# Counting every transfer in the planner's estimate of the DMA queue, turning the first x + h first, and turning part of the attention scores by DMA

## The chip, the cores and the metric

The kernel runs on one core of one Trainium2 chip. Its time is the device time of one execution in microseconds (us). The kernel before was timed three times: 1010.28, 1007.97 and 1010.57 us, median 1010.28 us. One execution was recorded with a profile; durations below come from that one.

The core has these engines: PE (TensorE) multiplies matrices and writes to PSUM, which is read by DVE (VectorE) and ACT (ScalarE); POOL (GpSimd) does a few casts at the start; SP (SyncE) computes nothing, it issues every transfer (DMA) of this kernel. Each engine takes its own instructions strictly in the order in which they were written, and waits at an instruction until what that instruction needs is there.

## The reference

There are eight batches of 3136 rows (keys and queries at once) and 256 columns.

```python
scores = (1/S) * z @ z.T            # z: 8 x 3136 x 64, so scores are symmetric
attn   = maximum(scores, 0) ** 2
x      = u * (attn @ v)             # u, v: 8 x 3136 x 256
h      = (x.T @ U @ V).T            # U: 3136 x 32, V: 32 x 3136
y      = x + h
out    = y + maximum(y @ w_ch1, 0) @ w_ch2    # 256 -> 1024 -> 256
```

The scores of a batch are a 3136 x 3136 symmetric matrix. A block of it that is needed with keys and queries exchanged can therefore be had in two ways: compute it a second time on PE, or transpose (turn) the block that is there.

## The kernel before, in words

**Tiling.** 3136 rows are 24 tiles of 128 rows and one tail of 64. Four tiles make a group of 512, so a batch has six full groups (0 to 5) and a seventh item for the tail. `items` (L56) lists (batch, group): 56 items, t = 7b + g. The kernel works on one item after the other; item (b,g) is the attention output of query group g of batch b.

**What an item does on PE.** `av_stream` (L501) multiplies the scores of all 24 key tiles with v, block by block: `lhs(h, q, jt)` fetches the piece of the score block (b, g, jb), jb = jt // 4. Between these matmuls `emit` (L857) mixes other work at given places: score blocks of later items (`score_burst`), the mixer of an item that lies eight items back (`ch1_part`, `ch2_stream`), and `u2_unit` (L661), which makes y = x + h of the item seven back. `av_end` (L599) adds the part of the 64 tail keys. PE therefore always has work of three kinds: attention, scores, mixer. `pair` (L159, the matmul is L164) issues two matmuls of 64 rows, one on each half of PE's rows.

**Score blocks.** A block is 512 keys by 512 queries, 128 partitions x 2048 in bf16, and lives in one of 20 buffers (`take_block`, `give_block`). For query group g the blocks with J >= g are computed (two bursts of a pair of 64x512 matmuls, `score_pairs` L349; then ReLU with scale, `rectify` L317, on ACT or DVE; then `square` L313 on DVE). The blocks with J < g are turned by DMA from the block (b, J, g) computed earlier (`issue_turn` L336, the transfer is L341). The scores of the 64 tail keys against 512 queries are computed too: one burst ("last") for every two groups, in `last_sb`. Those of the tail queries against all keys are made in `score_small` (L416).

**x + h.** `u2_unit` makes y on DVE in 32 bits (L708), casts it to bf16 (`cast` L181, on whichever of ACT and DVE is free first by the plan), and turns it by DMA (`x_turn` L621, transfer L624) into `u2T`, which `ch1_part` reads one item later.

**The planner.** The order of all instructions is fixed when the program is written, by a plan kept beside it. `clock` counts PE's work (one unit for a pair of 256 columns); `free_at` holds when ACT, DVE and SP will be free by this plan; `hold` keeps work back until its due time, and `run_held` (L109) issues it. Turns that could go wait in `ready_turns`; `run_held` issues one when `free_at["sp"] <= now`, in the order of the group that needs it (J first). Before the change only the turns of blocks are booked on SP (34 units each, L345); loads, stores and the turns of x + h are not. A turn that is still in `ready_turns` when its block is wanted is issued there and then, by the loop in `lhs` (L509 to L513).

**SP's queue.** On SP stand, in the order in which they were written: at the end of item t the store of the output (`ch2_out`, L832), which waits for the last DVE result of the mixer of that item; at the start of the next item the load of u (L278, or L283 for the tail's 64 rows) and one or two loads of v (L227) or of z; then turns of blocks (L341) and the turn of x + h (L624). Only the order on SP and the data that a transfer needs decide when it starts: where in PE's stream it was written does not hold it.

Of the kernel before, what the change touches and what calls it, by code (L numbers as in the profile page):

```python
# [18 lines left out]
def kernel(  # L19
# [79 lines left out]
    unturned = {}  # L99
    ready_turns = []  # L100

    def book(eng, ready, cost):
        free_at[eng] = max(free_at[eng], ready) + cost
        return free_at[eng]

    def hold(due, f):
        held.append((due, len(held), f))

    def run_held(now=None):  # L109
        now = clock[0] if now is None else now  # L110
        while True:
            ripe = [h for h in held if h[0] <= now]
            if not ripe:
                break
            h = min(ripe, key=lambda e: (e[0], e[1]))
            held.remove(h)
            h[2]()
        while ready_turns and free_at["sp"] <= now:
            issue_turn(min(ready_turns, key=lambda e: (e[0], e[2], e[1])))
# [77 lines left out]
    def load_tail(raw, c0, a, n):  # L197

        for h in range(2):
            nc.sync.dma_start(out=raw[h * TAIL : (h + 1) * TAIL, c0 : c0 + n], in_=a[NF * P : S, :])  # L200


    def load_z_piece(b, t0, n, raw, tail=True):
        m = min(n, NF - t0)
        nc.sync.dma_start(  # L205
            out=raw[:, : m * dqk].rearrange("p (t d) -> p t d", d=dqk), in_=rows_of(z[b])[:, t0 : t0 + m, :]
        )
        if n > m and tail:
            load_tail(raw, m * dqk, z[b], dqk)
            load_tail(raw, n * dqk, v[b], D)  # L210
# [15 lines left out]
    def load_v_piece(b, k, raw):  # L226
        nc.sync.dma_start(  # L227
            out=raw.rearrange("p (t d) -> p t d", d=D), in_=rows_of(v[b])[:, k * GT : (k + 1) * GT, :]
        )

    def v_copy(b, k, raw, copy):
# [42 lines left out]
    def load_u(b, g):  # L274
        g0, gw = groups[g]
        t = pool.tile([P, GT, D], FP32, name="u_sb", bufs=2)
        if gw >= P:
            nc.sync.dma_start(  # L278
                out=t[:, : gw // P, :],
                in_=rows_of(u[b])[:, g0 // P : (g0 + gw) // P, :],  # L280
            )
        else:
            nc.sync.dma_start(out=t[:gw, 0, :], in_=u[b, g0 : g0 + gw, :])  # L283
        u_sbs[b, g] = t


    def z_turn_dma(b):
        nc.sync.dma_start_transpose(
            out=zzTs[b], in_=z_bfs[b].rearrange("p t c d -> p (t c d)")
        )  # L290

    def z_turn(b, t0, copy):
# [17 lines left out]
    def half(zzT, jj, c0, n):  # L310
        return zzT.rearrange("p t c -> p (t c)")[jj * dqk : (jj + 1) * dqk, c0 : c0 + n]

    def square(a, cost=6.3):  # L313
        book("dve", clock[0], cost)
        nc.vector.tensor_tensor(out=a, in0=a, in1=a, op=ALU.mult)  # L315

    def rectify(dst, src):  # L317

        ready = clock[0] + 3
        if max(free_at["dve"], ready) + 8 < max(free_at["act"], ready):  # L320
            nc.vector.tensor_scalar(  # L321
                out=dst, in0=src, scalar1=scale, scalar2=0.0, op0=ALU.mult, op1=ALU.max
            )
            return book("dve", ready, 11.2)
        nc.scalar.activation(out=dst, in_=src, func=AF.Relu, scale=scale)  # L325
        return book("act", ready, 8.7)

# [5 lines left out]
    def made_twice(b, g, J):  # L333
        return b == 0 and (g <= FIRST or J == g - 1)

    def issue_turn(e):  # L336
        ready_turns.remove(e)
        J, g, b = e
        src = blocks[b, g, J]
        blocks[b, J, g] = take_block()  # L340
        nc.sync.dma_start_transpose(  # L341
            out=blocks[b, J, g][1].rearrange("p j (q c) -> p (j q) c", c=P),
            in_=src[1].rearrange("p j c -> p (j c)"),
        )
        book("sp", clock[0], 34)  # L345
        if unturned.pop(src[0]):
            free_blocks.append(src[0])

    def score_pairs(jobs):  # L349

        made = []
        for b, g, job in jobs:
            zzT = zzTs[b]
            k, ps = take_ps()
            if job == "last":
                keys, cols = [NF, NF], [groups[g + jj][0] for jj in range(2)]
            else:
                J, h = job
                keys, cols = [J * GT + 2 * h + jj for jj in range(2)], [groups[g][0]] * 2
            pair(  # L360
                k,
# [4 lines left out]
                        dict(  # L366
                            out=ps[:, jj, :],
                            lhsT=half(zzT, jj, keys[jj] * P, P),
                            rhs=half(zzT, jj, cols[jj], GW),
                            start=True,  # L370
# [4 lines left out]
                ],  # L375
                GW,
            )
            if job == "last":
                lasts[b, g // 2] = pool.tile([P, 2, GW], BF16, name="last_sb")
                made.append((lasts[b, g // 2], k, ps, None, None))  # L380
                continue
            if h == 0:
                blocks[b, g, J] = take_block()
            made.append(
                (
# [9 lines left out]
    def score_finish(made):  # L395
        for dst, k, ps, turn, key in made:
            if turn:
                J, g, b = turn
                unturned[blocks[b, g, J][0]] = False
# [10 lines left out]
            hold(done, finish)  # L410

    def score_burst(jobs):
        score_finish(score_pairs(jobs))


    def score_small(b, g):  # L416
# [7 lines left out]
        for p0 in range(0, npair, per):  # L424
            n = min(per, npair - p0)
            pk, ps = take_ps()
            for k in range(n):
# [7 lines left out]
                                out=ps[:, jj, k * gw : (k + 1) * gw],  # L435
                                lhsT=half(zzT, jj, (2 * (p0 + k) + jj) * P, P),
                                rhs=half(zzT, jj, g0, gw),
# [63 lines left out]
    def av_stream(b, g, box):  # L501
        def lhs(h, q, jt):
# [12 lines left out]
            if jb >= g or made_twice(b, g, jb):  # L515
                while squared.get((b, g, jb), 0) < 2:
                    run_held(min(h[0] for h in held))
                return t[h, j, q * P : (q + 1) * P]

# [32 lines left out]
    def av_small(b, g):  # L552
# [3 lines left out]
        for jt in range(NT):  # L556
            c = jt % 2
            for h in range(2):
                nc.tensor.matmul(  # L559
                    out=ps[c * hp : c * hp + rows, h, :D],  # L560
                    lhsT=smalls[b][h * hp : (h + 1) * hp, jt, :],
                    rhs=v_bfs[b][h * hp : (h + 1) * hp, jt, :],
                    start=(jt < 2),
                    stop=(jt >= NT - 2),
                    tile_position=(h * hp, c * hp),
                )
# [32 lines left out]
    def av_end(b, g, box):  # L599

        last = lasts[b, g // 2]
        for a in range(2):
# [6 lines left out]
                        out=four(box["ps"])[:, q, :],  # L609
                        lhsT=last[h, g % 2, q * P : (q + 1) * P],  # L610
                        rhs=v_bfs[b][h, NF, :],
# [9 lines left out]
    def x_turn(b, g, turned):  # L621
# [4 lines left out]
            in_=xs[b, g][:rows, :n, :].rearrange("p q d -> p (q d)"),  # L626
        )


# [31 lines left out]
    def u2_unit(b, g, turn=True):  # L661
# [51 lines left out]
        def turned():  # L713
            u2Ts[b, g] = u2T_tile()
            x_turn(b, g, u2Ts[b, g])

        def down():
            hold(cast(x, o[:rows, :n, :], n * D) + 2, turned)

        hold(done - 3, down)  # L720

# [101 lines left out]
    def ch2_out(b, g, acc):  # L823
# [7 lines left out]
        dst = rows_of(out[b])[:, t0 : t0 + n, :] if rows == P else out[b, t0 * P : S, None, :]  # L831
        nc.sync.dma_start(out=dst, in_=o)  # L832
        if (b, g) in o_blocks:
            give_block(o_blocks.pop((b, g)))
# [71 lines left out]
    def jobs_of(b, g):  # L906
        js = [J for J in range(NQ) if J >= g or made_twice(b, g, J)]
        j = [(b, g, (J, h)) for J in js for h in range(2)]
        if g % 2 == 0:
            j.append((b, g, "last"))  # L910
# [5 lines left out]
    def load_U():  # L916
        entry, raw = stage_block()
        nc.sync.dma_start(out=raw[:, : NF * R].rearrange("p (t r) -> p t r", r=R), in_=rows_of(moe_U))
        nc.sync.dma_start(out=raw[:TAIL, NF * R : NT * R], in_=moe_U[NF * P :, :])

        def casts():
# [6 lines left out]
    def load_w(k):  # L928
        def step(i):
# [4 lines left out]
            else:  # L934
# [3 lines left out]
                )  # L938
                dst = w2_bf[:, i * GT : (i + 1) * GT, :].rearrange("p t d -> p (t d)")

            def casts(entry=entry, raw=raw, dst=dst):
# [8 lines left out]
    def load_V(i0):  # L950
        n = P // 4

        def step(i):
            entry, raw = stage_block()
            w = n * NF + (S - NF * P if i == 3 else 0)
            for c in range(NREP):
                nc.sync.dma_start(out=raw[c * R : (c + 1) * R, :w], in_=moe_V[:, i * n * NF : i * n * NF + w])

            def casts(i=i, entry=entry, raw=raw):
# [103 lines left out]
    for b in range(B):  # L1063
        for g in range(NQ):
# [8 lines left out]
            elif b == 0 and g == 0:  # L1073
                todo[0] += new[4:]
            else:
                todo[t] += new
# [6 lines left out]
    for t in range(n_items):  # L1083
# [30 lines left out]
        if t <= NG:  # L1114
            hold(clock[0] + 60, lambda t=t: load_u(*items[t + 1]))
        if b_next < B and g_now == 2:
            while spare:
# [18 lines left out]
        full = mix and mix[1] < NQ  # L1136
        if av and g_now == NQ - 1:
            qm.append((55, 2, False, lambda: score_small(att[0], NQ)))
        if av and full:
# [36 lines left out]
        if av and u2i:  # L1176
            if u2i[1] == 0:
                qm.append((8, 1, False, lambda: t1_all(u2i[0])))
            qm.append((34 if u2i[1] == 0 else 40, 1, False, lambda: u2_unit(*u2i)))

# [72 lines left out]
```

## Time and profile before

| what | us |
|---|---|
| runs without profile | 1010.28, 1007.97, 1010.57 |
| the profiled execution | 1010.08 |
| its span, first to last instruction | 1008.3 |
| PE busy | 986.7 |
| DVE busy | 653.6 |
| ACT busy | 520.2 |

The profile names a group of instructions by its line in the kernel, its engine, and "out<-in" by the names of the tiles. "idle before, releaser" says how long the engine stood still before that group and what ended it. PE is busy nearly all of the span. In the steady part a batch takes 121.66 us: the same pieces of the chain that ended last come back at 224.32, 345.98, 467.64 us and so on. The first batch has no mixer work; the last items have no scores.

### The profile page before, as it was taken

Reading aid. Unit: us, or ns where it says so; the run is one execution under the profiler, and the core shown is the slowest. Engines: PE = TensorE matmul, PEld = TensorE weight load, DVE = VectorE, ACT = ScalarE, POOL = GpSimd, SP = SyncE. Lnnn points to the kernel's source line nnn. Section 1 sums busy time; section 2 is a strip of 40 time slices with the busy share of each in tenths; the row PEclk is TensorE's granted clock in tenths of the full one; section 3 lists DMA queues with packets and bytes.
Section 4 is the critical chain, followed back from the end, with each engine's and each line's share of the span. In section 5 each row is a group of like instructions: output and inputs, shape, how many; then the busy total and the mean of one; then the engine's idle time right before and its main releaser. Section 6 shows DMA issues by size and latency. Waiting matters only on the chain.

```text
span 1008.3 us, 35337 instructions
## 1 busy us (share of the span) xinstructions
PE 986.7 (98%) x16179; PEld 784.7 (78%) x16179; DVE 653.6 (65%) x820; ACT 520.2 (52%) x599; POOL 17.2 (2%) x24
## 2 busy tenths in 40 slices
PE   6999899999999999999999999999999999999997
PEld 3898688877787777778777877778777777787776
DVE  5986675668666685666756677566776667653453
ACT  6896653357524573355733456444653356522453
POOL 4100000000000000000000000000000000000000
PEclk9999899999999999999999999999999999999999
DMA  7997998478966799568995789846798577873142
GB/s 247 187 257 178 235 170 166 130 166 186 213 142 165 152 199 218 149 145 181 182 209 157 129 193 188 210 127 140 179 216 185 137 158 143 160 127 88 45 103 94
DMA packets 337061, 167.84 MB, mean 166 GB/s; under 512 B 312336, under 2 KB 315408, under 8 KB 336912
## 3 DMA queue, kind: packets, MB, share of 16 engines
q1 hardware_dynamic: 336912, 165.59, 76.3%
q8 instruction: 126, 2.06, 0.8%
q14 instruction: 23, 0.19, 0.1%
HBM read 62.56 MB, written 25.69 MB: 88 GB/s over the span
## 4 chain that ended last, share of the span: by engine, by line
PE 94%; DVE 2%; ACT 2%; DMA 1%; issue 0%; POOL 0%; SPq 0%; POOLq 0%; ACTq 0%
PE ps L164 92%; PE ps L559 1%; DVE blk L315 1%; ACT blk L793 1%; PE ps L635 1%; DMA blk<-in_v_dram 1%; ACT blk L325 1%; PE ps L843 0%; DMA u2T<-x_bf 0%; DMA stage<-in_v_dram 0%; POOL z_bf L213 0%; SPq L205 0%; DVE blk L321 0%; DVE out_sb L708 0%; DVE blk L830 0%
## 5 line engine op out<-in xcount | busy, mean ns | idle before, releaser
L164 PEld LDWEIGHTS <-blk 64*128 64x128 bf16 x12288 | 617.6, 94 | 153.6 <-POOLq L154 8.7
L164 PE MATMUL ps<-v_bf,blk 64*128 64x256 bf16 x9216 | 617.2, 270 | 2.3 <-DVE blk L315 1.8
L325 ACT ACTIVATE blk<-ps 128x1024 bf16<-128x1024 f32 x324 | 323.4, 1027 | 337.2 <-PE ps L164 334.0
L315 DVE TENSOR_TENSOR blk<-blk 128x1024 bf16<-128x1024 bf16 x352 | 237.7, 701 | 34.1 <-ACT blk L325 33.4
L164 PE MATMUL ps<-u2T,w_bf 64*128 64x512 bf16 (+1 forms) x1792 | 239.1, 351 | 4.3 <-DMA u2T<-x_bf 3.5
L164 PE MATMUL ps<-w_bf,blk 64*128 64x256 bf16 x3072 | 193.7, 269 | 0.2
L790 DVE TENSOR_SCALAR blk<-ps 128x1024 bf16<-128x1024 f32 x96 | 115.7, 1205 | 102.3 <-PE ps L164 102.3
L793 ACT ACTIVATE blk<-ps 128x1024 bf16<-128x1024 f32 (+1 forms) x128 | 107.3, 847 | 82.4 <-PE ps L164 74.1
L164 PE MATMUL ps<-zzT 64*128 64x512 bf16 (+1 forms) x944 | 143.5, 342 | 1.9 <-ACT zzT L305 1.7
L164 PEld LDWEIGHTS <-w_bf 64*128 64x128 bf16 x1792 | 91.6, 94 | 35.1 <-DMA u2T<-x_bf 3.8
L592 DVE TENSOR_TENSOR x_bf<-ps,u_sb 128x1024 bf16<-128x1024 f32 x48 | 58.8, 1224 | 63.0 <-PE ps L164 62.9
L708 DVE TENSOR_TENSOR out_sb<-ps,x_bf 128x1024 f32<-128x1024 f32 (+1 forms) x49 | 54.3, 1107 | 53.7 <-PE ps L164 53.6
L830 DVE TENSOR_TENSOR out_sb<-ps,out_sb 128x1024 f32<-128x1024 f32 x42 | 51.3, 1222 | 18.3 <-PE ps L164 18.3
L164 PEld LDWEIGHTS <-zzT 64*128 64x128 bf16 x944 | 43.9, 95 | 9.2 <-ACT zzT L305 2.2
L325 ACT ACTIVATE last_sb<-ps 128x1024 bf16<-128x1024 f32 x23 | 23.5, 1024 | 26.5 <-PE ps L164 26.5
L321 DVE TENSOR_SCALAR blk<-ps 128x1024 bf16<-128x1024 f32 x24 | 29.4, 1224 | 10.3 <-PE ps L164 8.7
L186 DVE CAST x_bf<-out_sb 128x1024 bf16<-128x1024 f32 x33 | 22.8, 690 | 0.5
L186 DVE CAST v_bf<-stage 128x1024 bf16<-128x1024 f32 (+1 forms) x34 | 21.2, 626 | 0.0
L164 PE MATMUL ps<-t_sb,V_bf 64*128 64x256 bf16 x200 | 20.8, 269 | 0.0
L164 PE MATMUL ps<-v_bf,last_sb 64*128 64x256 bf16 x192 | 18.6, 269 | 0.0
L830 DVE TENSOR_TENSOR blk<-ps,blk 128x1024 f32<-128x1024 f32 x6 | 7.3, 1225 | 16.0 <-PE ps L164 15.9
L578 ACT COPY u_sb<-ps 64x512 f32<-64x512 f32 x8 | 4.7, 582 | 23.9 <-PE ps L559 23.9
(67 smaller groups left out, 249.5 us busy)
## 6 DMA issues: line engine op xcount, KB each, us to landing
u_sb<-in_u_dram SPq DMA_DIRECT2D x48, 512.0 KB, 5.0
stage<-in_v_dram SPq DMA_DIRECT2D x42, 512.0 KB, 6.0
out_dram<-out_sb SPq DMA_DIRECT2D x42, 512.0 KB, 3.1
stage<-in_z_dram SPq DMA_DIRECT2D x7, 512.0 KB, 5.5
blk<-in_v_dram SPq DMA_DIRECT2D x6, 512.0 KB, 7.2
out_dram<-blk SPq DMA_DIRECT2D x6, 512.0 KB, 2.6
blk<-in_moe_w_ch_dram SPq DMA_DIRECT2D x4, 512.0 KB, 5.8
stage<-in_z_dram SPq DMA_DIRECT2D x7, 256.0 KB, 5.7
```

What stands on the lines that cost most here:

```text
L164: ins = nc.tensor.matmul(**args)
L186: nc.vector.tensor_copy(out=out, in_=in_)
L315: nc.vector.tensor_tensor(out=a, in0=a, in1=a, op=ALU.mult)
L321: nc.vector.tensor_scalar(out=dst, in0=src, scalar1=scale, scalar2=0.0, op0=ALU.mult, op1=ALU.max)
L325: nc.scalar.activation(out=dst, in_=src, func=AF.Relu, scale=scale)
L559: nc.tensor.matmul(out=ps[c * hp : c * hp + rows, h, :D], lhsT=smalls[b][h * hp : (h + 1) * hp, jt, :], rhs=v_bfs[b][h * hp : (h + 1) * hp ...
L592: nc.vector.tensor_tensor(out=xs[b, g][:rows, :n, :], in0=four(box["ps"])[:rows, :n, :], in1=u_sbs[b, g][:rows, :n, :], op=ALU.mult,)
L635: nc.tensor.matmul(out=pt[c * R : (c + 1) * R, 0, :D], lhsT=U_bf[:rows, it, :], rhs=xs[b, g][:rows, q, :], start=(it < NREP), stop=(it + N ...
L708: nc.vector.tensor_tensor(out=o[:rows, :n, :], in0=four(ps)[:rows, :n, :], in1=x, op=ALU.add)
L790: nc.vector.tensor_single_scalar(out=r, in_=ps[:, :, :gw], scalar=0.0, op=ALU.max)
L793: nc.scalar.activation(out=r, in_=ps[:, :, :gw], func=AF.Relu)
L830: nc.vector.tensor_tensor(out=o, in0=acc, in1=o, op=ALU.add)
```

## The change: what it does

1. **Every transfer is booked on SP in the plan.** `queued(kb, turned)` adds 15 units per 512 KB of an ordinary transfer and 17 per 256 KB of a turned one to `free_at["sp"]`; it is called beside each load, store, z turn and x + h turn. `run_held` issues a block's turn only when SP is free by this larger sum; a turn that is still held when its block is wanted goes by the loop in `lhs`, as before.
2. **First x + h.** For group 0 of each batch `u2_unit` stands at place 22 of the item and not at 34, its cast is always on DVE and right behind the sum, and while `urgent` is filled no block's turn is issued.
3. **Tail keys by turning.** For batches 1 to 7 the three "last" bursts fall away. `score_small` of a batch is made in the item before the batch begins, and `last_turn` turns 24 x 64 of its columns into `last_sb` by one DMA at the start of the batch (12 pieces of 128 x 128). The order of the tiles in `attn_small` is changed so that the halves fit (`place_of`).
4. **A quarter of each diagonal block by turning.** In the block (b, g, g), `split` for all but the first four groups of batch 0, the second burst computes 256 columns and not 512, with ReLU and square over half as much; the missing quarter is turned by a DMA of 4 pieces of 128 x 128 inside the block. That turn goes through `ready_turns` with J = g. In `lhs` PE's stream needs it from the third tile of the block on.

```diff
+    def queued(kb, turned=False):
+        book("sp", clock[0], kb * (17 / 256 if turned else 15 / 512))
...
-        while ready_turns and free_at["sp"] <= now:
+        while ready_turns and free_at["sp"] <= now and not urgent:
             issue_turn(min(ready_turns, key=lambda e: (e[0], e[2], e[1])))
...
     def issue_turn(e):
         ready_turns.remove(e)
         J, g, b = e
         src = blocks[b, g, J]
+        if J == g:
+            nc.sync.dma_start_transpose(
+                out=flat_of(src)[:, 3 * GW :].rearrange("p (n c) -> p n c", c=P),
+                in_=flat_of(src)[:, GW : 2 * GW],
+            )
+            book("sp", clock[0], 12)
+            split_turned.add((b, g))
+            return
...
+                if split(b, g, J) and h:
+                    width = hw
+                    cols = [c + hw for c in cols]
...
+    def score_finish_split(flat, k, ps, h, key):
+        if h:
+            done = rectify(
+                flat[:, 2 * GW : 3 * GW].rearrange("p (j c) -> p j c", c=hw), ps[:, :, :hw], 0.5
+            )
+            a, cost = flat[:, 2 * GW : 3 * GW], 3.7
...
+        def finish():
+            square(a, cost)
+            squared[key] = squared.get(key, 0) + 1
+            if not h:
+                b, g, J = key
+                hold(clock[0] + 7, lambda: ready_turns.append((J, g, b)))
...
+    def last_turn(b):
+        lasts[b] = last_tile()
+        nc.sync.dma_start_transpose(
+            out=lasts[b], in_=smalls[b][:, :NF, :].rearrange("p t c -> p (t c)")
+        )
+        book("sp", clock[0], 26)
...
+                if split(b, g, jb):
+                    while j >= 2 and q < 2 and (b, g) not in split_turned:
+                        if (g, g, b) in ready_turns:
+                            issue_turn((g, g, b))
+                        else:
+                            run_held(min(h[0] for h in held))
...
-            hold(done - 3, down)
+        if g == 0:
+            urgent.append((b, g))
+            nc.vector.tensor_copy(out=x, in_=o[:rows, :n, :])
+            hold(book("dve", done, 6.3) - 6, turned)
+        else:
+            hold(done - 3, down)
...
         nc.sync.dma_start(out=dst, in_=o)
+        queued(n * rows)
...
-        if g % 2 == 0:
+        if g % 2 == 0 and b == 0:
             j.append((b, g, "last"))
...
+        if g_now == 0 and t:
+            last_turn(att[0])
...
-        if av and g_now == NQ - 1:
-            qm.append((55, 2, False, lambda: score_small(att[0], NQ)))
+        if av and t == NQ - 2:
+            qm.append((55, 2, False, lambda: score_small(0, NQ)))
+        if av and g_now == NQ - 1 and b_next < B:
+            qm.append((55, 2, False, lambda: score_small(b_next, NQ)))
...
-            qm.append((34 if u2i[1] == 0 else 40, 1, False, lambda: u2_unit(*u2i)))
+            qm.append((22 if u2i[1] == 0 else 40, 1, False, lambda: u2_unit(*u2i)))
```

## The prediction

> **What bounds the kernel now.** I read the page's busy times first, then its costliest groups, the windows around the one long wait of PE, and last the timelines of SP and PE over one late item of a batch.
>
> Page before: engines, granted clock, and the groups of PE with waits (busy, mean ns of one | idle before, releaser).
>
> ```profile
> PE 986.7 (98%) x16179; PEld 784.7 (78%) x16179; DVE 653.6 (65%) x820; ACT 520.2 (52%) x599; POOL 17.2 (2%) x24
> PEclk9999899999999999999999999999999999999999
> ...
> L164 PE MATMUL ps<-u2T,w_bf 64*128 64x512 bf16 (+1 forms) x1792 | 239.1, 351 | 4.3 <-DMA u2T<-x_bf 3.5
> ...
> L164 PE MATMUL ps<-zzT 64*128 64x512 bf16 (+1 forms) x944 | 143.5, 342 | 1.9 <-ACT zzT L305 1.7
> ```
>
> PE bounds the kernel: less work on PE is time won, and a wait put into PE is time lost in full, since no other slack follows it. The 3.5 us is the only long wait after the start, the first turned x + h. The windows around it (us, PE, PEld, DVE, ACT, POOL busy, clock, DMA share, GB/s):
>
> ```profile
> 114.00:118.00 4.00, 0.84 (x16) 0.56 (x11) 1.83 (x3) 0.20 (x1) 0.00 (x0) 0.94 1.25 185
> 118.00:124.00 6.00, 5.62 (x42) 3.15 (x44) 0.06 (x1) 2.87 (x3) 0.00 (x0) 0.50 1.04 263
> ```
>
> After that wait PE ran at half clock for 6 us, so it cost 3.5 + 3.0 = 6.5 us.
>
> SP over the item (2,5), which begins on PE at 320.2 (start, length, "idle before"):
>
> ```profile
> 310.40 1.24 SPq L624 DMA_TRANSPOSE u2T<-x_bf  x1
> 314.47 1.84 SPq L341 DMA_TRANSPOSE blk<-blk  x1
> 321.66 0.34 SPq L832 DMA_DIRECT2D out_dram<-out_sb  x1
> 322.06 1.23 SPq L283 DMA_DIRECT2D u_sb<-in_u_dram  x1
> 323.33 0.58 SPq L227 DMA_DIRECT2D stage<-in_v_dram  x1
> 325.34 3.48 SPq L341 DMA_TRANSPOSE blk<-blk  x1
> 329.68 2.88 SPq L341 DMA_TRANSPOSE blk<-blk  x1
> ```
>
> SP stands idle until 321.66, because the store waits for the end of the item before; only then come the loads, and what stands behind them starts 3.7 us after the item's start (323.91). The waits of SP and the view of L341 give the two prices that matter:
>
> ```profile
> SPq L832 <- DVE out_sb L830: 148.0, 44, 8.2
> ...
> L341 SPq DMA_TRANSPOSE blk<-blk x112: 1522/2837/5305, 23.3 to 902.2; - x112
> ...
> DMA to landing us min/median/max: 4.2/5.2/8.3
> ```
>
> A turn takes SP 2.8 us (median) and lands 4.2 to 8.3 us after its start. PE in the same item:
>
> ```profile
> 320.20 0.60 PE L164 MATMUL ps<-v_bf,blk 64*128 64x256 bf16 x8
> ...
> 327.37 0.38 PE L164 MATMUL ps<-t_sb,V_bf 64*128 64x256 bf16 x4
> 327.59 1.04 PE L164 MATMUL ps<-v_bf,blk 64*128 64x256 bf16 x16
> ...
> 331.54 0.84 PE L164 MATMUL ps<-v_bf,blk 64*128 64x256 bf16 x12
> ```
>
> With T = 320.2: `u2_unit` is at T+7.2; by the plan's steps PE wants block 2 at T+5.5, block 3 right behind `u2_unit` (T+7.4), block 4 at T+11.3, and the turned quarter of block 5 at T+12.8. One item earlier `u2_unit` was at 308.00 and its turn started at 310.40, so x + h is ready 2.4 us after PE.
>
> **The change part by part.**
>
> *PE work removed.* 7 batches x 3 "last" bursts, one pair of 512 columns each (8 pairs took 1.73 us, 340.36 to 342.09: 0.216): 21 x 0.216 = 4.5 us. 44 diagonal blocks, half a pair each (16 pairs of 256 columns took 1.74 us: 0.109): 44 x 0.109 = 4.8 us. Together -9.3 us. The ReLUs (1.02 us) and squares (0.68) that go lie beside PE: nothing.
>
> *First x + h.* `u2_unit` stands 14 units (1.5 us) earlier; on SP one block's turn and the one of 12 pieces stand ahead of its turn from the tail's item on, in place of three blocks' turns (the last of them held SP for 4.64 us from 109.22); its cast, always on DVE (0.69 us), lies in that lead; the planned lead over its use grows from 38 to 66 units (4.1 to 7.2 us) against a landing of 4.4 us. I take the whole 6.5 us as gained, -6.5; the other end is 0.
>
> *Tail keys by one turn.* 12 pieces of 128 x 128 land in between 3.3 us (x + h, 8 pieces) and 5.2 us (a block, 16); `av_end` wants them 135 units, over 14 us, later: 0. Uncovered it would be up to 5.2 us a batch. `score_small` only moves by an item: 0.
>
> *The larger estimate.* Here the cost lies. By plan the loads and turns of a batch now sum to nearly the 1100 units that the batch lasts, so turns pile up in `ready_turns`, and J = 5 is served last. In batches 1 to 6 they are written only when `lhs` wants them, which puts them on SP behind the store and the loads of their own item. The changed program has on SP, for item (2,5):
>
> ```
> out_dram<-out_sb          store of item (2,4)
> u_sb<-in_u_dram, stage<-in_v_dram
> blk<-blk 16 pieces        (3,2,0), next batch
> blk<-blk 16 pieces        (2,5,2), wanted at T+5.5
> blk<-blk 16 pieces        (2,5,3), wanted at T+7.4
> u2T<-x_bf                 x + h, needs u2_unit
> blk<-blk 16 pieces        (2,5,4), wanted at T+11.3
> blk<-blk 4 pieces         quarter of (2,5,5), wanted at T+12.8
> ```
>
> Before, all of batch 2's turns stood at least 273 units (30 us) ahead of their use. I take 2.9 us of SP for a turn, 1.25 for x + h, 4.9 to landing (what the turn at 329.68 took). SP is free at T+3.7; a turn (b+1,2,0) starts at T+5.1, its source not being squared earlier (325.34); (b+1,3,0) at T+9.5 (329.68).
>
> - Batch 1 (2, 3, x, 4, quarter): block 2 starts 3.7, lands 8.6, PE waits 3.1. `u2_unit` 10.3, x ready 12.7, SP free 13.95, block 4 lands 18.85: shift in all 18.85 - 11.3 = 7.5.
> - Batch 2 (as above): block 2 starts 8.0, lands 12.9, wait 7.4; `u2_unit` 14.6, x 17.0, block 4 starts 18.25, lands 23.15: 11.9.
> - Batches 3 and 4 (next batch's turn, 3, x, 4, quarter): block 3 starts 8.0, lands 12.9: 5.5 each; block 4 follows in time.
> - Batch 5 (two of the next batch, x, 4): SP free at 12.4, x to 13.65, block 4 lands 18.55: 7.3.
> - Batch 6 (4 in time; then next, x, next, quarter): x ends 10.85, next turn 13.75, the quarter, a size the trace lacks, between 2.3 (shortest x + h turn) and 4.2; near the first, 2.4: 16.15 - 12.8 = 3.4.
> - Batch 7 has no next batch and no late turn. Two quarters (group 1 of batches 3 and 5) stand behind the tail's store: about 0.5 each, 1.0.
>
> Sum 42. What stands behind the waiting matmul on PE, mixer and scores alike, waits too; nothing makes it up.
>
> *Clock.* The wait of 3.5 us halved the clock and cost 3.0 us more. Batches 2 to 5 have waits well above that, 4 x 3.0; batches 1 and 6 (3.1 and 3.4) are at the edge, half of 2 x 3.0: 15 us; ends 0 and 18.
>
> The Trainium skill, "TensorE: Matmul & The Clock Gate", section "HAM oscillation — how this bites in real kernels", has no idle gap above about 3.4 us as its rule, and a free-running window. Our 3.54 us wait agrees. By it alone the waits of batches 1 and 6 would keep the clock and the time would be 3 us less, an estimate of 1048. It also speaks against this change, which makes one such gap a batch.
>
> *DMA load.* A steady batch turns 15 x 16 + 50 + 25 = 315 pieces; 36 are added (11%), beside an 80% share (80.6% from 221.66 to 343.32): at most 90%. Taken at 0 as the turns are spread; it is the reason for the upper rival.
>
> **Sum**, from the profiled execution's 1010.1 (median of the runs 1010.3): 1010.1 - 9.3 - 6.5 + 42 + 15 = 1051 us.
>
> **Rivals.**
>
> - *Same late turns, cheaper.* Landing 4.2, SP 1.9 us a turn (both seen on an idle queue: 314.47), clock kept: 6.25 + 9.55 + 2 x 3.8 + 5.55 + 2.35 = 31, so 994.3 + 31 = 1026. Against it: the turn behind a load took SP 3.48 us. 0.18.
> - *Dearer.* Landing 6.5 (one at 343.77 took 6.2, the longest 8.3) since the queue is fuller: 1.6 more on each of 7 landings in series, and 18 for the clock, with further waits in the items behind: 1066 to 1070. 0.13.
> - *First x + h still late* (that part doesn't do what it says): 1057. The DMA share there is above 1.0, which speaks for it; the fewer turns ahead against. 0.07.
> - *Faster: the late turns wait for nothing.* Then only the gains remain, 994 us. It decides at block 2 and 3 of items (b,5): started at T+3.7 they would have to land within 1.8 us, where 112 turns took 4.2 at least. Or the store would have to be ready 5 us sooner, but it ends on PE's own work. 0.05.
>
> **How the numbers follow.** My case has 0.56, own range 1040 to 1062; 0.01 lies between the cheap rival and the fast one. 0.3%, 3 us, is about what a measurement here can tell. Slower holds 0.94, faster 0.05, same 0.01. The range takes half of the cheap rival and half of the dear one: 1024 to 1068.
>
> **What would show it.** Right: PE idle "<-DMA blk<-blk" of some 40 us in five or six places, once a batch, in the item with group 5; the clock row with digits under 9 there; the wait for u2T gone; zzT matmuls down from 944 by 42, and 88 narrowed. SP would show L375 in place of L341 directly behind the loads of those items. Wrong: PE without waits in those items, or blocks landing before T+5.5.

## The result and the profile after

The changed kernel takes 1054.01 us (median of 4 runs, 1053.02 to 1055.29) where the kernel before, on the same chip, takes 1010.42 us (4 runs, 1007.97 to 1011.47): a ratio of 1.0436, interval 1.0418 to 1.0455. It is slower by 44 us; 1051 had been predicted, in a range of 1024 to 1068.

The profiled execution took 1054.05 us, its span is 1052.3 us. The diff moves the lines: the matmul, L164 before, is L169 now; the turn of a block, L341, is L375; the turn of x + h, L624, is L721; the store of the output, L832, is L936; the loads L227 and L283 are L234 and L291. L367 is new, the turn of a quarter.

First the page of the kernel after: the engines, the granted clock, the costliest groups of PE and the DMA queue (packets, MB, share of 16 engines).

```profile
PE 991.0 (94%) x16137; PEld 804.4 (76%) x16137; DVE 618.0 (59%) x793; ACT 491.4 (47%) x584; POOL 17.3 (2%) x24
...
PEclk9999999999998899999999999999999999999999
...
q1 hardware_dynamic: 371824, 174.12, 79.0%
...
L169 PE MATMUL ps<-v_bf,blk 64*128 64x256 bf16 x9216 | 629.2, 272 | 46.5 <-DMA blk<-blk 43.1
...
L169 PE MATMUL ps<-u2T,w_bf 64*128 64x512 bf16 (+1 forms) x1792 | 242.8, 353 | 0.2
...
L169 PE MATMUL ps<-zzT 64*128 64x512 bf16 (+2 forms) x902 | 135.4, 336 | 1.8 <-ACT zzT L315 1.7
```

Four things are to be seen. PE has 42 matmul instructions fewer, all of them score matmuls (944 to 902), and yet is busy for 4.3 us longer than before (991.0 against 986.7). The wait for the first x + h is gone (4.3 us of idle time before the u2T group, now 0.2). The attention matmuls, which waited for no turned block before, now wait 43.1 us for them. And the clock row has two eights. The DMA queue moves 174.12 MB, 165.59 before, and takes 79.0% of the 16 engines over the longer span (76.3% before).

The waits of PE for turned blocks (total us, times, longest) and of SP's queue for the store's data:

```profile
PE ps L169 <- DMA blk<-blk: 43.1, 12, 6.9
```

```profile
SPq L936 <- DVE out_sb L934: 189.6, 48, 12.7
```

Twelve waits, none over 6.9 us, make the 43.1. On SP the store stands still for 189.6 us in all, until the mixer's last result is there. This costs nothing by itself; it costs as soon as something that PE wants soon stands behind it. The timeline of SP over the item (2,5), whose attention begins at 324.98 (start, length, engine, line, operation):

```profile
326.45 0.34 SPq L936 DMA_DIRECT2D out_dram<-out_sb  x1
326.85 0.50 SPq L291 DMA_DIRECT2D u_sb<-in_u_dram  x1
327.40 0.68 SPq L234 DMA_DIRECT2D stage<-in_v_dram  x1
330.13 7.75 SPq L375 DMA_TRANSPOSE blk<-blk  x3
343.76 1.47 SPq L721 DMA_TRANSPOSE u2T<-x_bf  x1
345.32 1.84 SPq L375 DMA_TRANSPOSE blk<-blk  x1
347.22 1.84 SPq L367 DMA_TRANSPOSE blk<-blk  x1
```

The timeline of PE over the same item, the rows that matter (in brackets the idle time before, and what ended it):

```profile
324.98 0.62 PE L169 MATMUL ps<-v_bf,blk 64*128 64x256 bf16 x8
...
337.67 0.61 PE L169 MATMUL ps<-v_bf,blk 64*128 64x256 bf16 x4 [6.86 <-DMA blk<-blk]
...
340.63 0.63 PE L169 MATMUL ps<-t_sb,V_bf 64*128 64x256 bf16 x4
...
349.77 1.25 PE L169 MATMUL ps<-v_bf,blk 64*128 64x256 bf16 x10 [4.38 <-DMA blk<-blk]
```

Store, two loads, a turn for the next batch, and only then the turns that this item needs: block 2, the second turn in the L375 row at 330.13, lands at 337.62, 12.6 us after the item's start, and PE goes on at 337.67. `u2_unit` follows at 340.63; x + h is turned at 343.76, 3.1 us later, and the turn of block 4, which stands behind it, ends a second wait of 4.38 us. The windows around both waits (us, busy time of PE, PEld, DVE, ACT, POOL, granted clock, DMA share, GB/s):

```profile
330.80:337.70 6.90, 0.04 (x3) 0.04 (x4) 0.00 (x0) 1.02 (x1) 0.00 (x0) 0.76 1.07 184
337.70:341.20 3.50, 3.50 (x28) 2.00 (x30) 0.00 (x0) 1.02 (x1) 0.00 (x0) 0.50 0.56 104
...
349.80:354.90 5.10, 5.10 (x42) 2.94 (x44) 0.00 (x0) 1.62 (x2) 0.00 (x0) 0.50 0.00 0
```

After each of these two waits PE works at half clock for some microseconds. So a late turn can be paid twice: as idle time, and as busy time that grew.

### The profile page after: what moved, and what is told of

Read it like the earlier page. It is cut to its first block, busy times and chain, and to the rows that moved or that the text cites. A ratio compares the mean times of both kernels' runs of the same rounds, so it can differ in the third digit from the quotient of the medians.

```text
span 1052.3 us, 35355 instructions
## 1 busy us (share of the span) xinstructions
PE 991.0 (94%) x16137; PEld 804.4 (76%) x16137; DVE 618.0 (59%) x793; ACT 491.4 (47%) x584; POOL 17.3 (2%) x24
## 2 busy tenths in 40 slices
DMA packets 371974, 176.38 MB, mean 168 GB/s; under 512 B 347248, under 2 KB 350320, under 8 KB 371824
## 3 DMA queue, kind: packets, MB, share of 16 engines
q1 hardware_dynamic: 371824, 174.12, 79.0%
## 4 chain that ended last, share of the span: by engine, by line
PE 90%; DMA 5%; DVE 1%; SPq 1%; ACT 1%; issue 1%; POOL 0%; POOLq 0%; DVEq 0%; ACTq 0%
PE ps L169 87%; DMA blk<-blk 5%; PE ps L652 1%; SPq L375 1%; DVE blk L339 1%; PE ps L733 1%; ACT blk L349 1%; DMA blk<-in_v_dram 1%; PE ps L948 0%; ACT blk L897 0%; SPq L721 0%; POOL z_bf L220 0%; DVE blk L345 0%; DVE blk L934 0%; DVE out_sb L806 0%
## 5 line engine op out<-in xcount | busy, mean ns | idle before, releaser
L169 PEld LDWEIGHTS <-blk 64*128 64x128 bf16 x12288 | 636.9, 95 | 186.9 <-DMA blk<-blk 47.4
L169 PE MATMUL ps<-v_bf,blk 64*128 64x256 bf16 x9216 | 629.2, 272 | 46.5 <-DMA blk<-blk 43.1
L339 DVE TENSOR_TENSOR blk<-blk 128x1024 bf16<-128x1024 bf16 x352 | 226.2, 666 | 59.0 <-ACT blk L349 58.4
L169 PE MATMUL ps<-u2T,w_bf 64*128 64x512 bf16 (+1 forms) x1792 | 242.8, 353 | 0.2
L894 DVE TENSOR_SCALAR blk<-ps 128x1024 bf16<-128x1024 f32 (+1 forms) x110 | 127.1, 1156 | 119.9 <-PE ps L169 119.3
L169 PE MATMUL ps<-w_bf,blk 64*128 64x256 bf16 x3072 | 194.4, 269 | 0.2
L897 ACT ACTIVATE blk<-ps 128x1024 bf16<-128x1024 f32 (+1 forms) x114 | 97.6, 866 | 91.5 <-PE ps L169 88.4
L169 PE MATMUL ps<-zzT 64*128 64x512 bf16 (+2 forms) x902 | 135.4, 336 | 1.8 <-ACT zzT L315 1.7
L169 PEld LDWEIGHTS <-w_bf 64*128 64x128 bf16 x1792 | 96.3, 95 | 26.9 <-POOLq L159 4.1
L169 PEld LDWEIGHTS <-zzT 64*128 64x128 bf16 x902 | 44.8, 97 | 8.9 <-ACT zzT L315 2.2
L169 PE MATMUL ps<-t_sb,V_bf 64*128 64x256 bf16 x200 | 21.4, 272 | 0.0
L189 ACT CAST x_bf<-out_sb 128x1024 bf16<-128x1024 f32 (+1 forms) x21 | 17.3, 826 | 6.0 <-DVE out_sb L806 6.0
L169 PE MATMUL ps<-v_bf,last_sb 64*128 64x256 bf16 x192 | 19.1, 271 | 0.0
L345 DVE TENSOR_SCALAR blk<-ps 128x1024 bf16<-128x1024 f32 (+1 forms) x9 | 10.0, 1106 | 13.5 <-PE ps L169 13.5
L189 ACT CAST v_bf<-stage 128x1024 bf16<-128x1024 f32 x15 | 15.6, 1041 | 0.0
L673 DVE TENSOR_TENSOR u_sb<-ps,u_sb 64x512 f32<-64x512 f32 x8 | 5.5, 682 | 17.1 <-ACT u_sb L671 17.1
```

The lines of the kernel that those rows point to most:

```text
L169: ins = nc.tensor.matmul(**args)
L189: nc.scalar.copy(out=out, in_=in_)
L894: nc.vector.tensor_single_scalar(out=r, in_=ps[:, :, :gw], scalar=0.0, op=ALU.max)
L897: nc.scalar.activation(out=r, in_=ps[:, :, :gw], func=AF.Relu)
```

## The experiments

Each ratio compares a kernel with the kernel before, timed beside it on the same chip; the median of the kernel before was 1007.67, 1007.69 or 1008.89 us there (1010.42 us in the result above), so a difference of 1 or 2 us between two experiments says little.

### The booking taken out

```diff
     def queued(kb, turned=False):
-        book("sp", clock[0], kb * (17 / 256 if turned else 15 / 512))
+        pass
```

> The changed kernel, only that the loads, stores and turns of z and of x + h are again not booked on SP (queued does nothing); block turns, quarters and the turn of the tail keys are still there and booked. My theory, that the written order on SP makes the blocks late: in the program every block's turn then stands at least 80 units (8.7 us) ahead of its use, so PE's waits for blk (43.1 us) and their half clock (about 14 us) go and the gains stay: 994 to 999 us. Rival, that the added turns overfill the DMA engines (79.0% against 76.3%) whatever the order: 1030 us or more, with PE still waiting for blk.

Measured: 1015.5 us (10 runs, 1012.24 to 1022.03), ratio 1.0071 [1.0049, 1.0093]. Neither expectation came true. The block waits are gone altogether, which the theory said, but another wait came. Groups of the trace of this kernel:

```profile
L169 PE MATMUL ps<-u2T,w_bf 64*128 64x512 bf16 (+1 forms) x1792 | 237.7, 351 | 19.3 <-DMA u2T<-x_bf 19.1
```

The turned x + h is late, 11 times, up to 4.48 us, and the longest wait, ending at 157.76, is followed by a stretch at half clock. SP's timeline before that:

```profile
139.22 8.18 SPq L297 DMA_TRANSPOSE zzT<-z_bf  x1
147.50 2.26 SPq L375 DMA_TRANSPOSE blk<-blk  x1
149.86 1.33 SPq L367 DMA_TRANSPOSE blk<-blk  x1
151.29 3.02 SPq L375 DMA_TRANSPOSE blk<-blk  x1
154.37 1.30 SPq L721 DMA_TRANSPOSE u2T<-x_bf  x1
```

SP has no gap there. The x + h that PE wants next was cast by 143.55 us, and its turn starts only at 154.37, behind the z turn, two blocks' turns and a quarter's. PE does not want the blocks and the quarter for a long time (the least lead of a turn over its use, counted in the order in which the instructions are written, is 80 units or 8.7 us, a quarter; blocks have more). So the booking does have work to do in this kernel: it keeps turns that have time from standing in front of x + h. Taking it out moves the lateness from the blocks to x + h.

### The booking alone, and the first x + h alone

The kernel before with part 1 only (`queued` and its ten calls):

```diff
+    def queued(kb, turned=False):
+        book("sp", clock[0], kb * (17 / 256 if turned else 15 / 512))
```

> The kernel before with part 1 of the change alone: every transfer is booked on SP, nothing else changes. If the estimate is harmful by itself: PE waits for blk in group 5 as in the changed kernel, 1040 to 1055 us. My theory, that it harms only with the 44 quarters and 7 tail turns booked on top (they bring the plan's sum for SP to the length of a batch): every turn stands 118 units or more ahead, no waits for blk, 1007 to 1013 us.

Measured: 1002.68 us (7 runs, 1001.74 to 1003.42), ratio 0.9945 [0.9924, 0.9965]: faster than before. Both expected ranges missed: the theory was right that no block waits, but it did not see a gain. The waits of its PE for x + h, the timeline of its SP where the first x + h was late, and that of the kernel before:

```profile
PE ps L167 <- DMA u2T<-x_bf: 0.3, 1, 0.3
```

```profile
107.07 1.94 SPq L349 DMA_TRANSPOSE blk<-blk  x1
109.09 1.70 SPq L632 DMA_TRANSPOSE u2T<-x_bf  x1
```

```profile
109.22 4.64 SPq L341 DMA_TRANSPOSE blk<-blk  x1
113.96 1.25 SPq L624 DMA_TRANSPOSE u2T<-x_bf  x1
```

Before, a block's turn of 4.64 us stood at 109.22 and x + h came at 113.96. With the larger estimate that turn is held back, x + h goes at 109.09, and its 3.5 us wait and the half clock behind it are gone. No block is late: without the quarters and the tail's turn in the estimate, the least lead is 118 units, 12.9 us. The same estimate that makes the changed kernel slow makes the kernel before faster.

The kernel before with part 2 only:

```diff
-        while ready_turns and free_at["sp"] <= now:
+        while ready_turns and free_at["sp"] <= now and not urgent:
...
-        hold(done - 3, down)
+        if g == 0:
+            urgent.append((b, g))
+            nc.vector.tensor_copy(out=x, in_=o[:rows, :n, :])
+            hold(book("dve", done, 6.3) - 6, turned)
+        else:
+            hold(done - 3, down)
...
-            qm.append((34 if u2i[1] == 0 else 40, 1, False, lambda: u2_unit(*u2i)))
+            qm.append((22 if u2i[1] == 0 else 40, 1, False, lambda: u2_unit(*u2i)))
```

> The kernel before with part 2 of the change alone: u2_unit of group 0 at place 22, its cast on DVE, no block's turn while its turn is awaited. If that removes the wait for the first turned x + h (3.5 us and 3.0 us of half clock): 1002 to 1005 us, as the estimate alone does. If the turns that held SP there are not written by this and the wait stays: 1008 to 1011 us.

Measured: 1007.32 us (10 runs, 1002.66 to 1008.69), ratio 0.9983 [0.9962, 1.0005]. The profiled execution (1004.03 us) shows the first wait gone, and one of 0.6 us left elsewhere; but the runs spread over 6 us, their median lies between the two expected ranges, and the interval includes no change at all. Whether part 2 alone is worth the 6.5 us is left inconclusive.

### The late turns put ahead of the store

The changed kernel, estimate and all, but before the last unit of the mixer of an item, so ahead of its store, every turn that is ready and that the next item needs is issued:

```diff
             light = av.units[: nA - 8] + ch2[: nC // 2] + av.units[nA - 8 :] + ch2[nC // 2 :]
+
+            def ahead(b=att[0], g=att[1] + 1, f=light[-1]):
+                for e in sorted(e for e in ready_turns if e[0] == g and e[2] == b):
+                    issue_turn(e)
+                f()
+
+            light[-1] = ahead
```

> The changed kernel with its full estimate, but before the last unit of an item, which writes the store, all turns that are ready and that the next item wants are issued, so that they stand on SP ahead of the store and the loads. My theory: the waits in group 5 of batches 1 to 6 go (39 us and about 13 us of half clock), the one at 98 us in batch 0 (2.7 and 1.7 us) stays, since no store stands there: 999 to 1006 us. Rival of the full DMA engines: as many turns are moved by the same engines, 1030 us or more.

Measured: 999.71 us (5 runs, 998.65 to 1002.9), ratio 0.9922 [0.9895, 0.9949], as the theory said. What is left of the waits for blocks:

```profile
PE ps L169 <- DMA blk<-blk: 6.4, 4, 2.3
```

The same transfers under the same estimate, and 54 us less than the changed kernel: being held back costs little, standing behind the store and the loads of the own item costs nearly all. Of the four waits that are left the longest, 2.34 us, is the one in batch 0.

### The order of the ready turns

The key by which a ready turn is chosen puts the batch first and not the group:

```diff
-            issue_turn(min(ready_turns, key=lambda e: (e[0], e[2], e[1])))
+            issue_turn(min(ready_turns, key=lambda e: (e[2], e[0], e[1])))
```

> The changed kernel with one key exchanged: among the ready turns the present batch goes ahead of the next batch, then the group. The estimate is as large as in the changed kernel. My theory: behind the loads of item (b,5) only blocks 3 and 4 and the quarter of batch 1 and block 4 and the quarter of batch 2 are left, with nothing of the next batch ahead of them: about 1.2 us of waits in batch 1, 1 to 2 us for quarters of group 1 behind the store in some batches, the wait in batch 0 stays: 1000 to 1008 us. If the place behind the store alone decided, and not what stands ahead of them there, batches 1 and 2 would keep most of their 7 and 11 us: 1020 us. Rival of the full DMA engines: 1030 us or more.

Measured: 999.59 us (4 runs, 997.31 to 1000.25), ratio 0.9907 [0.9876, 0.9938], just under the expected range. The waits of its PE for blocks:

```profile
PE ps L169 <- DMA blk<-blk: 4.6, 3, 3.2
```

The longest of the three, 3.23 us, is again in group 5 of batch 1 (about 1.2 us were expected there); the other two are under 1 us, and in batches 2 to 6 group 5 waits no more. So it took two things to make group 5 late in every batch: a plan in which SP is full, and an order by group, in which the next batch's turns for group 0 overtake this batch's for group 5.

### No quarters

```diff
     def split(b, g, J):
-        return J == g and not (b == 0 and g <= FIRST)
+        return False
```

> The changed kernel without part 4: no diagonal block is split, so its second burst is whole again and no quarter is turned; the full estimate, the first x + h and the turned tail keys stay. In the program one turn alone is late: block 4 for item (1,5), behind the loads of its item, two turns of the next batch and the turn of x + h. My theory prices it by the sum of batch 5 in the prediction: one wait of about 7 us near 210 us, and a half clock behind it of about 3; no other wait for blk. From the kernel with the estimate alone (1002.7 us): - 4.5 (21 bursts) + 10 = 1006 to 1010 us. Rival, that any added turn brings waits in every batch: 1015 us or more.

Measured: 1006.47 us (10 runs, 1003.85 to 1007.28), ratio 0.9981 [0.9964, 0.9998]. The waits of PE for blocks, and the windows of the one wait that is left:

```profile
PE ps L169 <- DMA blk<-blk: 6.0, 1, 6.0
```

```profile
202.20:208.20 6.00, 0.00 (x1) 0.00 (x0) 0.99 (x1) 0.61 (x3) 0.00 (x0) 0.67 1.01 187
208.20:211.00 2.80, 2.80 (x26) 1.81 (x28) 0.00 (x0) 1.02 (x1) 0.00 (x0) 0.50 0.00 0
```

One late turn, that of block 4 of item (1,5), costs 6.0 us of idle time. The 2.8 us of work at half clock behind it would take half as long at full clock, so they cost 1.4 us more, not 3. The quarters are booked with 12 units each, 72 in a batch of about 1100: with them PE waits twelve times, without them once.

### The size of the estimate

```diff
-        book("sp", clock[0], kb * (17 / 256 if turned else 15 / 512))
+        book("sp", clock[0], 0.75 * kb * (17 / 256 if turned else 15 / 512))
```

> The changed kernel with loads, stores and the turns of z and x + h booked at three quarters of the change's price. By the plan SP then has room in every batch; the least lead of a turn in the program is 49 units (5.4 us), most over 100. My theory, by now that the estimate has to lie between two failures (none at all: x + h is turned late, 19.1 us of waits; full: blocks are turned late, 43.1 us): neither is late, 995 to 1000 us. If x + h is late here as without the estimate: 1005 to 1015 us. If blocks stay late: 1020 us or more.

Measured: 993.17 us (4 runs, 991.62 to 994.18), ratio 0.9857 [0.9841, 0.9873]: faster than both kernels, and a little under the expected range. Its page, and the largest of its PE waits behind the start:

```profile
PE 974.1 (98%) x16137; PEld 783.7 (79%) x16137; DVE 618.3 (62%) x793; ACT 491.5 (50%) x584; POOL 17.2 (2%) x24
```

```profile
PE ps L169 <- ACT v_bf L189: 1.8, 1, 1.8
```

PE waits for no transfer any more, neither block nor x + h. The comparison with the changed kernel closes the account of the late turns: PE is busy 991.0 - 974.1 = 16.9 us longer there with the same number of matmul instructions, and idle for 43.1 us behind blocks; the sum, 60.0, is the difference of the spans (1052.3 - 992.4 = 59.9).

The other way, the factor 1.25 in that line:

```diff
-        book("sp", clock[0], kb * (17 / 256 if turned else 15 / 512))
+        book("sp", clock[0], 1.25 * kb * (17 / 256 if turned else 15 / 512))
```

> The changed kernel with the other transfers booked at one and a quarter of the change's price; the transfers themselves are the same. By the plan SP is then over full in every batch, and in the program the turns of groups 1 to 5 of nearly every batch are written only where PE wants them, behind the loads of their item. My theory: waits for blk in five items of each batch, not one, each some 5 to 11 us with its half clock: 1200 to 1350 us. If lateness is set by the DMA engines and not by the written order: no more than the 1054 us of the changed kernel, since the same bytes move.

Measured: 1584.68 us (2 runs, 1580.57 and 1588.79), ratio 1.5713 [1.5642, 1.5784]. Engines, clock and the wait:

```profile
PE 1094.4 (69%) x16137; PEld 799.9 (50%) x16137; DVE 619.3 (39%) x793; ACT 494.4 (31%) x584; POOL 17.2 (1%) x24
...
PEclk9998788887788878787888887887888788887899
```

```profile
PE ps L169 <- DMA blk<-blk: 474.2, 62, 14.4
```

The same transfers, the same bytes (176.38 MB), and 474.2 us of waits in 62 places. The direction was expected, the size was not, by more than 230 us. With it falls the rival that the load on the DMA engines, and not the written order, makes blocks late: the bytes are unchanged, and the queue's share of the 16 engines is 48.3%, the lowest of all.

Both remedies together, batch first and a factor of 0.9:

```diff
-            issue_turn(min(ready_turns, key=lambda e: (e[0], e[2], e[1])))
+            issue_turn(min(ready_turns, key=lambda e: (e[2], e[0], e[1])))
...
-        book("sp", clock[0], kb * (17 / 256 if turned else 15 / 512))
+        book("sp", clock[0], 0.9 * kb * (17 / 256 if turned else 15 / 512))
```

> Both remedies: the present batch's turns ahead of the next batch's, and the price of the other transfers at nine tenths. The least lead in the program is 20 units for one quarter in batch 1 (2.2 us), else 57 and more. Expected: the 3.2 us wait at 200 us and its half clock, which were left with the order alone, go: 994 to 998 us; if x + h becomes late again: over 1000 us.

Measured: 993.03 us (4 runs, 991.46 to 994.86), ratio 0.9861 [0.9846, 0.9876]: the same as with 0.75 alone, and 1 us under the expected range. With no DMA wait left, the order has nothing more to give.

The points with parts 2 to 4 in place and the order by group:

| factor on the estimate | us | PE waits for blocks | for x + h |
|---|---|---|---|
| 0 | 1015.5 | 0 | 19.1 |
| 0.75 | 993.2 | 0 | 0 |
| 1 | 1054.0 | 43.1 | 0 |
| 1.25 | 1584.7 | 474.2 | 0 |

### What part 2 is worth, where nothing else waits

The kernel with 0.75, without the early place, the cast on DVE and `urgent`:

```diff
-        if g == 0:
-            urgent.append((b, g))
-            nc.vector.tensor_copy(out=x, in_=o[:rows, :n, :])
-            hold(book("dve", done, 6.3) - 6, turned)
-        else:
-            hold(done - 3, down)
+        hold(done - 3, down)
...
-            qm.append((22 if u2i[1] == 0 else 40, 1, False, lambda: u2_unit(*u2i)))
+            qm.append((34 if u2i[1] == 0 else 40, 1, False, lambda: u2_unit(*u2i)))
```

> The kernel with the price at three quarters (993.2 us), without part 2: u2_unit of group 0 back at place 34, its cast on ACT or DVE by the plan, block turns not held back for it. If the estimate alone keeps the first turned x + h early, as in the kernel with the estimate alone: 992 to 996 us, no wait for u2T. If part 2 is what does it: a wait for u2T near 115 us and its half clock, 997 to 1001 us.

Measured: 1003.89 us (8 runs, 1002.64 to 1005.09), ratio 0.9957 [0.9942, 0.9972], 10.7 us more than with part 2. The waits of PE for x + h:

```profile
PE ps L169 <- DMA u2T<-x_bf: 8.8, 5, 2.4
```

The five stand at about 237, 359, 480, 603 and 725 us: in group 0 of batches 2 to 6. The very first x + h, near 115, waits for nothing. Both expectations looked at that one place and missed; part 2 pays in the later batches, and the estimate pays in the first.

## Why the prediction was right

*PE work removed, -9.3.* With no DMA wait left (factor 0.75) the same pieces of the chain come back every 120.10 us (217.61, 337.71, 457.81), where a batch took 121.66 before: 1.56 us a batch, 10.9 over seven. By the prediction's prices a full batch loses 3 x 0.216 + 6 x 0.109 = 1.30, so it was 0.26 short. PE's busy time tells which part of this is work: it fell from 986.7 to 974.1 us, and 3.0 of these 12.6 us are the half clock of the kernel before; 9.6 us are left, close to the 9.3 predicted. The other 1.3 of the 10.9 us are idle time; which waits they were is not shown.

*First x + h, -6.5.* The wait is gone, as predicted. The cause given was incomplete: the steps named were those of part 2, but part 1 alone removes the wait too (0.3 us are left of it), and in the profiled execution of part 2 alone it is gone as well.

*Tail keys by one turn, 0.* No wait of the changed kernel is for `last_sb`: right.

*The late turns, 42.* Measured in the trace after, item by item:

| item | predicted | idle behind blocks |
|---|---|---|
| batch 1, group 5 | 7.5 | 0.94 + 2.37 + 1.60 + 2.43 = 7.3 |
| batch 2, group 5 | 11.9 | 6.86 + 4.38 = 11.2 |
| batch 3, group 5 | 5.5 | 5.1 |
| batch 4, group 5 | 5.5 | 5.4 |
| batch 5, group 5 | 7.3 | 6.2 |
| batch 6, group 5 | 3.4 | 4.1 |
| quarters of group 1, batches 3 and 5 | 1.0 | 1.0, at one place |
| sum | 42 | 40.4 |

The steps hold one by one in (2,5), with T = 324.98: SP free at T+3.1 (predicted 3.7), the turn for the next batch at T+5.15 (5.1), block 2 landed at T+12.6 (12.9), x + h turned 3.1 us behind `u2_unit` (2.4), and block 4 landed at T+24.7 (23.15). The two that are later stand behind the half clock, which the prediction had put in a term of its own. A quarter's turn, which the trace before lacked, is seen in the view of its line (instructions, then us to landing):

```profile
L367 SPq DMA_TRANSPOSE blk<-blk x44: 1189/1218/2502, 69.9 to 958.4; - x44
...
DMA to landing us min/median/max: 2.4/3.3/5.6
```

It was taken at 2.4, its least; the median is 3.3, but the quarter that PE waits for in batch 6 took 2.5. In batch 1 the sum of 7.5 was met by luck: 0.94 us of the 7.3 are a turn that stood ahead of the store, and block 3, which was to be in time, cost 1.60.

*Clock, 15.* The trace after has seven stretches at half clock. The sum of their windows (us, busy time of the engines):

```profile
sum 37.55, PE 28.76 PEld 18.07 DVE 2.02 ACT 9.32 POOL 0.00; mean PE 4.11 PEld 2.58 DVE 0.29 ACT 1.33 POOL 0.00
```

At full clock the 28.76 us of work would have taken half as long, so the half clock cost 14.4 us. Of these 1.7 lie in batch 0, below; 12.7 are left, 11.2 in batches 2 to 5 (12 predicted) and 1.5 in batches 1 and 6 (3 predicted): batch 1 kept its clock, batch 6 lost it. PE's busy time grew by more, 16.9 us; the other 2.5 us lie outside these stretches, and what they are is not shown.

*Not foreseen: a quarter late in batch 0, 4.4 us.* SP and PE there:

```profile
87.73 4.75 SPq L375 DMA_TRANSPOSE blk<-blk  x1
92.53 0.57 SPq L234 DMA_DIRECT2D stage<-in_v_dram  x1
93.20 1.15 SPq L291 DMA_DIRECT2D u_sb<-in_u_dram  x1
94.39 1.27 SPq L367 DMA_TRANSPOSE blk<-blk  x1
```

```profile
98.02 0.61 PE L169 MATMUL ps<-v_bf,blk 64*128 64x256 bf16 x7 [2.73 <-DMA blk<-blk]
...
117.17 1.05 PE L169 MATMUL ps<-v_bf,blk 64*128 64x256 bf16 x16 [1.77 <-ACT v_bf L189]
```

The quarter of (0,5,5) goes at 94.39, behind a turn that held SP for 4.75 us and two loads; PE waits 2.73 us and loses 1.7 us more to the clock (3.41 us of work at half clock from 98.89). The prediction looked at batches 1 to 7 alone. The second row is a cast of v that now goes to ACT and is waited for (0.52 us on DVE before): the factor 0.75 keeps this wait.

*The sum.* 1010.1 - 10.9 - 6.5 + 1.3 (the cast) = 994.0, which is what the kernel with 0.75 takes (994.18 in its profiled execution); 43.1 of idle time and 16.9 of longer busy time on top make 1054.0. So each term holds within some 2 us, but that 1051.3 lacks only 2.7 us is in part luck: 4.4 in batch 0, 1.3 of the cast and 2.5 of busy time outside the half clock were not in the sum; against them the clock cost 2.3 and the late turns 1.6 less than predicted, and 1.6 more was gained in place of the 9.3.

*The rivals.* "Cheaper", with its 4.2 us to landing, was nearer to the landings than the main case with its 4.9. The turns of blocks that item (2,5) has behind its loads:

```profile
DMA to landing us min/median/max: 4.4/4.5/4.9
```

The blocks that PE waited for behind the loads of their item landed after 4.4 to 4.5 us in batches 2 to 5, and after 6.1, 6.1 and 4.4 us in batch 1. "Cheaper" falls at the sum of the waits (40.4 us, not 31) and at the clock, which did drop. "Dearer" falls by the same landings: only two of them are near its 6.5 us. "First x + h still late" and "faster" are refuted by the trace itself. The faster one was right in one point: the time without late turns, 994, is that of the kernel with 0.75.

## What to carry to other kernels

A planner's estimate of a shared queue that works strictly in order had its best value here between two failures: too small, and eager transfers stand in front of the urgent one; too large, so that the bookings sum to the length of the round, and transfers are held until they are wanted and then stand behind a store that waits for the end of the work before. Judge it by what stands ahead of a transfer in the written order, and by what that waits for, not by bytes or by the share of busy DMA engines: one of the two fastest kernels here (factor 0.75, 993 us) has the busiest queue, 87.2%, the slowest (factor 1.25) has 48.3%. And price a wait of PE with the half clock behind it: here 14.4 us on 43.1.

## What the runs showed of the hardware that was not expected

*The clock changes on a fixed grid, and a wait's place on it decides.* All fourteen changes of the granted clock in the trace after, from 98.89 to 866.89 us, lie at 98.89 + n x 3.413 us (n = 0, 1, 69, 71, 73, 75, 110, 111, 147, 149, 186, 188, 224, 225). A stretch at half clock lasts one or two steps of this grid here, 3.41 or 6.83 us; with the factor 1.25 up to five, 17.07 us. Three steps of the grid in the kernel after (us, busy time of PE, PEld, DVE, ACT, POOL, granted clock, DMA share, GB/s):

```profile
95.48:98.89 3.41, 0.87 (x13) 0.55 (x15) 0.06 (x1) 0.01 (x1) 0.00 (x0) 1.00 1.13 294
204.70:208.11 3.41, 1.91 (x26) 1.19 (x26) 0.01 (x1) 1.16 (x2) 0.00 (x0) 1.00 0.79 172
208.12:211.53 3.41, 1.87 (x30) 1.39 (x32) 2.49 (x4) 0.57 (x1) 0.00 (x0) 1.00 0.00 0
```

The 2.73 us wait, from 95.29 to 98.02, lies almost wholly in the step from 95.48 to 98.89 (2.54 of its 3.41 us are idle), and the clock halves at the end of the step, 0.9 us after PE had gone on. The waits of 2.37 and 2.43 us, in batch 1, lie across a grid line (204.70 and 214.94); no step there has more than 1.54 us idle (208.12), and the clock stays. That is why batch 1 paid nothing for its clock.

The other traces bring the limit closer. Without the quarters a step with 2.00 us idle is followed by half clock; with the factor 1.25 one with 1.85 us idle is followed by full clock:

```profile
200.79:204.20 3.41, 1.41 (x22) 0.86 (x18) 1.68 (x2) 2.02 (x6) 0.00 (x0) 1.00 0.96 181
```

```profile
85.23:88.64 3.41, 1.56 (x28) 1.11 (x22) 3.41 (x5) 1.02 (x1) 0.00 (x0) 1.00 0.89 165
```

No step of the twelve traces, behind the first 20 us, contradicts this: at full clock all with 2.00 us idle or more lose it, and all with 1.85 or less keep it. At half clock PE must be busier to get it back: after at most 0.7 us idle in a step the clock was full again, after 0.8 us or more it stayed at half (the nearest pair, with the factor 1.25: 0.71 us in the step from 464.10, and 0.79 us in the one from 747.41). So what counts here is how much of one step is idle, and not how long one wait is.

The Trainium skill, "TensorE: Matmul & The Clock Gate", section "🔬 Part 1: The HAM clock gate (the "warmup" mystery)", gives a free-running window of 4096 cycles at 1.2 GHz, 3413 ns: the grid of 3.413 us agrees. The Trainium skill, same page, section "HAM oscillation — how this bites in real kernels", has no idle gap above about 3.4 us as its rule. Here shorter gaps, 2.73 us and, with the late turns put ahead of the store, 2.34 us (2.11 of them in one step, 95.18 to 98.59), already cost the clock, and the measurement decides.

*A small turn is not small on SP.* A quarter has 4 pieces where a block has 16, but takes SP 1.2 us against 2.3 (medians in the trace after), and lands in 3.3 us against 5.2. One long turn holds SP more than any of them: the z turn took it for 8.18 us at 139.22 in the kernel without the booking.
